# Turning the tokens of an expert's block on VectorE, from rows fetched by quarters, in a fused attention and mixture-of-experts kernel

## The chip, the cores and the metric

The kernel runs on one core of one Trainium2 chip. The metric is the device time of one execution in microseconds (us), lower is better. A profile of one execution gives, beside it, what each engine did and when: PE (TensorE matmuls), PEld (its weight loads), DVE (VectorE), ACT (ScalarE), POOL (GpSimd) and SP (SyncE, which here only issues DMAs and reads registers).

## The reference

Causal attention over 8 batches, 8 heads, 576 positions and 64 features, with a bias from a cumulative sum; its output is read as 4608 tokens of 512 features and goes through a router that sends each token to one of 8 experts:

```python
logits = x @ w_gate + modality_bias[modality_id]
e_idx = np.argmax(logits, axis=1)
...
gate_w = probs[np.arange(N), e_idx]
for e in range(E):                                  # N, D, E, F = 4608, 512, 8, 1024
    mask = e_idx == e
    h = np.maximum(x[mask] @ w1[e], 0.0)
    out[mask] = gate_w[mask, None] * (h @ w2[e])
```

All numbers are float32.

## The kernel before

**Attention** (class `Attn`, some 376 us of the span). 32 pairs of (two batches, one head) are scored, exponentiated, turned and multiplied with V. For each two batches a row of 576 floats is kept per token: 512 features, then 64 floats whose first two become the gate weight and the token's number. Routing (`Route`) scatters the rows with indirect DMAs into `lists`, a DRAM array with a region for each expert, and makes tables on the chip: `t2` with 6 blocks whose lists are filled from the first three quarters of the tokens, `t3` with 12 more, `t4` with what is left over.

**Experts** (class `Moe`). `run` goes through 18 blocks of 256 tokens of one expert (`nu` = 2), then one double block of 64 + 64 tokens (`nu` = 0, function `two`), then a loop of 64-token blocks (`nu` = 1, `quarter`), which may be empty. Each number is carried as a high and a low part in fp32r, so each product is three matmuls. For each 256-token block:

- `gather` fetches its 256 rows from `lists` into tile `xg` ([128, 2, 576], two buffers) and adds a table's entry to the token's number for the scatter at the end (`oi`, L1027).
- `xt` turns them, so that the features lie on partitions: eight TensorE transposes of 128x128 (L1039) into two PSUM tiles `tp` of one bank; for each, ACT copies the high part into `xT` (L1041) and DVE makes the low part (L1042).
- `block` makes the first layer: four groups `hp` of 24 matmuls (L1089, 256 columns), each emptied by ACT (`hT`, high, L1091) and DVE (`hT`, low, L1092); `hp` has two buffers.
- `second` makes the second layer: 48 matmuls of 512 columns into two tiles `y` (L1064); ACT (L1074) and DVE (L1072) multiply them by the gate weight from `xg` into `ys`, and POOL scatters `ys` to the output (L1075).

The weights of a block are eight chunks of 512 KB (`fetch`, L940 for w1 and L942 for w2) into six raw buffers (`wraw`, `wrbw`); ACT makes the high part (L965) and DVE the low part (L966) in 13 buffers (`wca`, `wcb`, `wcc`).

**The order.** Everything is written out in program order and each engine runs its own queue in order. While block k is multiplied, `pre(k+1)` issues the gather of block k+1 and its first two weight chunks; each of the eight `step()` calls in the block issues one more. `mid()` stands between the two layers of block k and holds `xt` of block k+1. For block 0 `xt` runs in `pre(0)`, ahead of everything else of the experts. After `xt` of block 0 the rest of the routing is emitted (`routed`), and after block 2 begins, the tables `t3` and `t4` (`R.rest`, on DVE).

All DMAs of gather and weights are issued by SP, in program order:

```python
xg, oi = self.gather(tb, b, r, nu)
x = self.xt(xg, nu) if k == 0 else None
W, self.more = self.weights(e, ...) 
```

The host passes `w1` with its 512 rows in an order that matches how `xt` takes features from the row.

Of the kernel before, what the change touches and what calls it, by code (L numbers as in the profile page):

```python
# [7 lines left out]
F32 = mybir.dt.float32  # L8
F32R = mybir.dt.float32r
BF16 = mybir.dt.bfloat16  # L10
I32 = mybir.dt.int32
AF = mybir.ActivationFunctionType
ALU = mybir.AluOpType
# [4 lines left out]
P = 128  # L18
KW = 576
XW = 72  # L20
# [18 lines left out]
class Attn:  # L39
# [166 lines left out]
    def rows(self, ho):  # L206

        nc = self.nc
        for a, (m, l) in enumerate(((0, 512), (64, 0))):
            for o, i in ((self.QL[0][64:74, a, m:m + 512].rearrange("p (c q) -> p c q", c=4), ho[64:74, :4].unsqueeze(2).broadcast_to([10, 4, P])),  # L210
                         (self.QL[0][64:74, a, l:l + 64], ho[64:74, 4:5].broadcast_to([10, 64]))):
                if a:
                    with self.tc.issue_after(self.last):
                        self.last = nc.gpsimd.tensor_scalar(o, i, 1.0, 1.0, ALU.mult, ALU.mult).ins
                else:
                    with self.tc.issue_after(self.act):
                        self.act = nc.scalar.copy(o, i).ins
# [688 lines left out]
class Moe:  # L906
# [95 lines left out]

    def gather(self, tb, b, r, nu):
        nc = self.nc
        xg = self.mx.tile([P, nu or 1, XW // 2, 8, 2], F32, name=f"xg{nu or 1}", bufs=2)
        if nu == 0:
            i = [nc.sync.dma_start(xg[64 * q:64 * q + 64, 0].rearrange("p d h r -> p (d h r)"), self.R.lists[bass.ds(r[q], 64), :]).ins for q in range(2)]
        elif nu == 2:
            i = nc.sync.dma_start(xg.rearrange("p u d h r -> p u (d h r)"),
                                  self.R.lists[bass.ds(r, 2 * P), :].rearrange("(u p) d -> p u d", u=2)).ins  # L1010
        else:
            i = nc.sync.dma_start(xg[:64, 0].rearrange("p d h r -> p (d h r)"), self.R.lists[bass.ds(r, 64), :]).ins
        if tb is self.R.t2:
            self.R.nodep(i, self.R.scat[27:])
            need = self.R.scat[:27]
        else:
            need = self.R.scat
        for i, o in ((i, o) for i in (i if nu == 0 else [i]) for o in need):
            self.tc.add_manual_dep(i, o.name, mybir.DependencyInfo(mybir.DependencyClass.Sync, mybir.DependencyReason.DATA), reason="rows of the list")
        oi = self.mp.tile([P, 2], I32, name="oi", bufs=3)  # L1020
        if nu == 0:
            for q in range(2):
                r = slice(64 * q, 64 * q + 64)
                nc.vector.tensor_tensor(oi[r, :1], xg[r, :1, 32, 0, 1], tb["past"][r, b + q], ALU.add)
            return xg, oi
        n = P if nu == 2 else 64
        nc.vector.tensor_tensor(oi[:n, :nu], xg[:n, :nu, 32, 0, 1], tb["past"][:n, bass.ds(b, 1), :].rearrange("p b u -> p (b u)"), ALU.add)  # L1027
        return xg, oi

    def xt(self, xg, nu):  # L1030
        nc = self.nc
        if nu < 2:
            return self.xq(xg) if nu else self.x2(xg)
        xT = self.mp.tile([P, 2, 4, 256], F32R, name="xT")
        for g in range(2):
            tp = self.ps.tile([P, 2, 256], F32, name="tp")
            for k in range(2):
                for u in range(2):
                    tr = nc.tensor.transpose(out=tp[:, k, P * u:P * u + P],  # L1039
                                        in_=xg[:, u, 16 * g + 8 * k:16 * g + 8 * k + 8].rearrange("p d h r -> p (d h r)"), identity=self.ident)  # L1040
            hi = nc.scalar.copy(xT[:, 0, 2 * g:2 * g + 2], tp)  # L1041
            lo = nc.vector.tensor_tensor(xT[:, 1, 2 * g:2 * g + 2], tp, xT[:, 0, 2 * g:2 * g + 2].bitcast(F32), ALU.subtract)  # L1042
        self.tr = (tr, hi, lo)
        return xT
# [13 lines left out]
    def second(self, W, xg, oi, hT):  # L1058
        nc = self.nc
        y = [self.ps.tile([P, 512], F32, name="y") for _ in range(2)]  # L1060
        for f in range(8):
            for u in range(2):
                for i, (a, c) in enumerate(self.PASS):
                    self.last[0] = nc.tensor.matmul(y[u], hT[:, a, f, P * u:P * u + P], W[4 + f // 2][:, c, 512 * (f % 2):512 * (f % 2) + 512],  # L1064
                                                    start=f == 0 and i == 0, stop=f == 7 and i == 2)
            if f % 2:
                self.step()
        for u in range(2):
            ys = self.my.tile([P, 512], F32, name="ys", bufs=3)
            gate = xg[:, u, 32, 0, 0:1]  # L1070
            if u:
                self.last[1] = nc.vector.tensor_scalar(ys, y[u], gate, None, ALU.mult)  # L1072
            else:
                self.last[3] = nc.scalar.activation(ys, y[u], AF.Copy, scale=gate)  # L1074
            self.last[2] = nc.gpsimd.indirect_dma_start(  # L1075
                out=self.out, out_offset=bass.IndirectOffsetOnAxis(ap=oi[:, u:u + 1], axis=0),
                in_=ys, in_offset=None, bounds_check=4607, oob_is_err=False)

    def block(self, W, xg, oi, xT, mid):
# [16 lines left out]
        mid()  # L1096
        self.second(W, xg, oi, hT)

    def xq(self, xg):
        nc = self.nc  # L1100
        xT = self.mp.tile([P, 2, 4, 256], F32R, name="xT")[:, 0, :, :P]
        tp = self.ps.tile([P, 4, 64], F32, name="tp")
        for k in range(4):
            nc.tensor.transpose(out=tp[:, k], in_=xg[:64, 0, 8 * k:8 * k + 8].rearrange("p d h r -> p (d h r)"), identity=self.ident[:64, :64])
        nc.scalar.copy(xT[:, :, :64], tp)
        nc.vector.tensor_tensor(xT[:, :, 64:], tp, xT[:, :, :64].bitcast(F32), ALU.subtract)
        return xT
# [13 lines left out]
    def x2(self, xg):  # L1121
        nc = self.nc
        X = self.mp.tile([P, 2, 4, 256], F32R, name="xT")[:, 0]
        tp = self.ps.tile([P, 4, P], F32, name="tp")
        for k in range(4):
            nc.tensor.transpose(out=tp[:, k], in_=xg[:, 0, 8 * k:8 * k + 8].rearrange("p d h r -> p (d h r)"), identity=self.ident)
        self.split(X, tp)
        return X

# [264 lines left out]
```

## Time and profile before

| | us |
|---|---|
| median of 3 runs | 825.9 (825.75 to 826.71) |
| the profiled execution | 826.59, of which its span is 824.9 |
| attention, to the first transpose of a block | 0 to 376.7 |
| 18 blocks | 376.7 to 802 |
| double block and end | 802 to 824.9 |
| PE busy in the three | 371.64, 424.80, 16.52 |
| DVE busy in the three | 252.78, 276.41, 11.12 |

Busy times are sums of instruction durations merged where they overlap; matmuls are pipelined, so the time a matmul takes is longer than the distance to the next one. A row of a group reads: line, engine, operation, output <- inputs, shapes, count, busy us, mean ns of one, idle time before them and what ended it. Lines are those of the kernel before.

### The profile page before, as it was taken

The page shows a single profiled execution, that of the slowest core. Times are in us where ns is not written, and L with a number is a line of the kernel's source. Part 1 is how long each engine was busy: PE and PEld are TensorE (multiplying, and loading weights), DVE is VectorE, ACT ScalarE, POOL GpSimd, SP SyncE. Part 2 cuts the span into 40 slices and gives each one's busy share as a digit, 9 for nine tenths or more (in the row PEclk, how much of TensorE's full clock was granted, in tenths as well). Part 3 has the DMA queues.
Part 4 walks back from the last instruction along what each step waited for, and adds up shares of the span by engine and source line. Part 5 has one row for each costly group of instructions (what it writes and reads, how often), then busy time and mean ns, then how long its engine had stood idle before and what let it go on. Part 6 is the DMA issues. An engine that isn't in the chain of part 4 may idle for free. (4 is left out here: it accounts for less than half of the span.)

```text
span 824.9 us, 16646 instructions
## 1 busy us (share of the span) xinstructions
PE 813.0 (99%) x5692; PEld 699.1 (85%) x5692; DVE 540.3 (66%) x1405; ACT 530.5 (64%) x1196; POOL 359.2 (44%) x383
## 2 busy tenths in 40 slices
PE   7999999999999999999999999999999999999996
PEld 7878887888887788888888899998888999988884
DVE  7666666667766677766489865555566664556874
ACT  6888788878887788876265555444455554444663
POOL 8959778988699877992500000000000000000010
PEclk7999999999999999999999999999999999999999
DMA  7565556766566656737797866655556666555970
GB/s 235 164 205 182 180 181 196 238 226 196 171 188 225 210 158 219 226 106 286 251 380 277 303 259 259 245 210 198 209 196 234 259 259 250 200 205 210 370 247 29
DMA packets 68548, 182.31 MB, mean 221 GB/s; under 512 B 7993, under 2 KB 8889, under 8 KB 68334
## 3 DMA queue, kind: packets, MB, share of 16 engines
q1 hardware_dynamic: 62622, 161.17, 57.4%
q0 software_dynamic: 5840, 20.06, 6.2%
q8 instruction: 46, 0.75, 0.4%
q14 instruction: 40, 0.33, 0.1%
HBM read 144.73 MB, written 26.80 MB: 208 GB/s over the span
## 5 line engine op out<-in xcount | busy, mean ns | idle before, releaser
L1075 POOL DMA_INDIRECT out<-ys,oi x36 | 35.9, 997 | 368.4 <-ACT ys L1074 298.5
L396 DVE CUSTOM_DVE_ANT_0 pe<-sp,mk 128x512 f32<-128x512 f32 (+3 forms) x256 | 122.4, 488 | 100.4 <-PE sp L394 92.3
L416 ACT ACTIVATE pe<-pe,mx 128x512 f32<-128x512 f32 (+3 forms) x256 | 144.3, 565 | 16.5 <-DVE mx L396 13.8
L433 PE MATMUL pt<-ident,pe 128*128 128x128 f32 x640 | 111.9, 281 | 0.1
L437 ACT COPY PT<-pt 128x512 f32<-128x512 f32 (+1 forms) x192 | 97.0, 508 | 21.2 <-PE pt L433 21.2
L372 PE MATMUL sp<-KA,QH 128*128 128x256 f32 (+2 forms) x256 | 102.6, 403 | 2.1 <-POOL KA L236 2.1
L1091 ACT ACTIVATE hT<-hp 128x512 fp32r<-128x512 f32 x72 | 42.8, 595 | 93.1 <-PE hp L1089 92.6
L474 PE MATMUL o<-PT,V 128*64 128x320 f32 (+4 forms) x896 | 100.7, 364 | 0.0
L474 PEld LDWEIGHTS o<-PT,V 128*64 128x64 f32 x896 | 58.6, 136 | 46.7 <-issue 14.7
L1089 PE MATMUL hp<-xT,wcb 128*128 128x256 f32 x648 | 89.6, 282 | 0.0
L1089 PE MATMUL hp<-xT,wca 128*128 128x256 f32 x624 | 87.3, 282 | 0.5 <-ACT xT L1041 0.5
L433 PEld LDWEIGHTS pt<-ident,pe 128*128 128x128 f32 x640 | 77.3, 145 | 12.2 <-issue 5.3
L326 POOL TENSOR_TENSOR KA<-rawk,KA 64x576 fp32r<-64x576 f32 x62 | 87.1, 1421 | 0.2
L326 POOL TENSOR_TENSOR QL<-rawq,QH 64x576 fp32r<-64x576 f32 x62 | 86.7, 1413 | 0.2
L394 PE MATMUL sp<-KB,QL 76*128 76x256 f32 (+2 forms) x256 | 85.9, 340 | 0.9 <-DMA QL<-ek 0.9
L1092 DVE SCALAR_TENSOR_TENSOR hT<-hp,hT 128x512 fp32r<-128x512 f32 x72 | 49.5, 688 | 53.2 <-ACT hT L1091 52.9
L1089 PEld LDWEIGHTS hp<-xT,wcb 128*128 128x128 f32 x648 | 83.1, 188 | 0.6
L1089 PEld LDWEIGHTS hp<-xT,wca 128*128 128x128 f32 x624 | 80.4, 188 | 1.4 <-issue 0.7
L1064 PE MATMUL y<-wcb,hT 128*128 128x512 f32 x336 | 81.2, 398 | 0.0
L1064 PEld LDWEIGHTS y<-wcb,hT 128*128 128x128 f32 x336 | 62.8, 188 | 14.7
L1089 PE MATMUL hp<-xT,wcc 128*128 128x256 f32 x456 | 64.6, 281 | 0.0
L1064 PE MATMUL y<-wca,hT 128*128 128x512 f32 x264 | 63.9, 398 | 0.0
(285 smaller groups left out, 1599.2 us busy)
## 6 DMA issues: line engine op xcount, KB each, us to landing
wrbw<-in_w SPq DMA_DIRECT2D x104, 512.0 KB
wraw<-in_w SPq DMA_DIRECT2D x56, 512.0 KB
rawq<-in_qkv SPq DMA_DIRECT2D x31, 576.0 KB
rawk<-in_qkv SPq DMA_DIRECT2D x31, 576.0 KB
xg<-lists SPq DMA_DIRECT2D x18, 576.0 KB
V<-in_qkv SPq DMA_DIRECT2D x32, 320.0 KB
KB<-KA SPq DMA_DIRECT2D x62, 144.0 KB
lists<-z SPq DMA_DIRECT2D x8, 576.0 KB
```

The costliest lines, as they stand in the source:

```text
L326: self.last = nc.gpsimd.tensor_tensor(o, i, h, ALU.subtract).ins
L372: self.pe.append(self.nc.tensor.matmul(sp[:, :nn], QH[:, q0:q0 + P], self.KA[u][:, ab, :nn], start=True, stop=False).ins)
L394: self.pe.append(nc.tensor.matmul(sp[:, :nn], QL[:EXT, q0:q0 + P], KB[:EXT, ab, :nn], start=False, stop=True).ins)
L396: ins = nc.vector.tensor_tensor_reduce(out=t[:, :n], in0=sp[:, :n], in1=self.mk[:, 512 - n:512], scale=-0.125, scalar=3.0e38, op0=ALU.add, ...
L416: self.act = nc.scalar.activation(t[:, :n], t[:, :n], AF.Exp, bias=m, scale=-1.0, accum_out=st["sums"][:, o:o + 1]).ins
L433: self.pe.append(nc.tensor.transpose(out=pt[:, o:o + P], in_=pe[:, P * j:P * j + P], identity=self.ident).ins)
L437: cp(w[:, :, :, v:v + P], pt[:, :n * (1 + both)].rearrange("p (a j q) -> p a j q", a=1 + both, q=P))
L474: m = nc.tensor.matmul(o[r, f - q0:q1 - q0], V[:, ab, j, :], PT[:, ab, PTS * j + f if j < 4 else PTW - 64:PTS * j + q1 if j < 4 else PTW], ...
L1064: self.last[0] = nc.tensor.matmul(y[u], hT[:, a, f, P * u:P * u + P], W[4 + f // 2][:, c, 512 * (f % 2):512 * (f % 2) + 512], start=f == 0 ...
L1089: nc.tensor.matmul(hp[:, u], W[k][:, a, f:f + P], xT[:, c, k], start=k == 0 and i == 0, stop=k == 3 and i == 2)
L1091: hi = nc.scalar.activation(hs, hp, AF.Relu)
L1092: lo = nc.vector.scalar_tensor_tensor(hT[:, 1, 2 * m:2 * m + 2], hp, 0.0, hs.bitcast(F32), ALU.max, ALU.subtract)
```

## The change

For 256-token blocks, `gather2` takes the place of the one DMA of `gather`. Four DMAs each fetch a quarter of the 512 features of all 256 tokens (512 bytes a token) onto 32 partitions: partition 32q + p holds, for t = 0 to 7, features 128q to 128q + 127 of token 32t + p (tile `xr`, [128, 8, 128], two buffers). A fifth DMA fetches two floats for each token, the gate weight and the number (tile `tg`, three buffers). In `xt` two VectorE instructions take the place of the eight transposes: each turns 32x32 blocks, reads every fourth feature and writes a whole `tp` tile. The gate weight and the number come from `tg`. The host orders the rows of `w1` so that feature 4d + k of a quarter meets its weight, and the transposes of the 64-token blocks (`x2`, `xq`, still on TensorE) read every fourth feature too. The 64-token gathers keep one DMA; their buffers are now of 576 floats, and `xg2` is gone.

```diff
     def gather(self, tb, b, r, nu):
         nc = self.nc
-        xg = self.mx.tile([P, nu or 1, XW // 2, 8, 2], F32, name=f"xg{nu or 1}", bufs=2)
+        if nu == 2:
+            return self.gather2(tb, b, r)
+        xg = self.mx.tile([P, 1, XW // 2, 8, 2], F32, name="xg", bufs=2)
...
-        elif nu == 2:
-            i = nc.sync.dma_start(xg.rearrange("p u d h r -> p u (d h r)"),
-                                  self.R.lists[bass.ds(r, 2 * P), :].rearrange("(u p) d -> p u d", u=2)).ins
...
+    def rows(self, tb, ins):
+
+        need = self.R.scat
+        if tb is self.R.t2:
+            for i in ins:
+                self.R.nodep(i, need[27:])
+            need = need[:27]
+        for i, o in ((i, o) for i in ins for o in need):
+            self.tc.add_manual_dep(i, o.name, ...)
+
+    def gather2(self, tb, b, r):
+
+        nc = self.nc
+        xr = self.mx.tile([P, 8, P], F32, name="xr", bufs=2)
+        tg = self.mx.tile([P, 2, 2], F32, name="tg", bufs=3)
+        rows = self.R.lists[bass.ds(r, 2 * P), :]
+        i = [nc.sync.dma_start(xr[32 * q:32 * q + 32], rows[:, P * q:P * q + P].rearrange("(t p) d -> p t d", p=32)).ins for q in range(4)]
+        i.append(nc.sync.dma_start(tg, rows[:, 512:514].rearrange("(u p) d -> p u d", u=2)).ins)
+        self.rows(tb, i)
+        oi = self.mp.tile([P, 2], I32, name="oi", bufs=3)
+        nc.vector.tensor_tensor(oi, tg[:, :, 1], tb["past"][:, bass.ds(b, 1), :].rearrange("p b u -> p (b u)"), ALU.add)
+        return (xr, tg), oi
 
     def xt(self, xg, nu):
...
         for g in range(2):
             tp = self.ps.tile([P, 2, 256], F32, name="tp")
-            for k in range(2):
-                for u in range(2):
-                    tr = nc.tensor.transpose(out=tp[:, k, P * u:P * u + P],
-                                        in_=xg[:, u, 16 * g + 8 * k:16 * g + 8 * k + 8].rearrange("p d h r -> p (d h r)"), identity=self.ident)
+            tr = nc.vector.transpose(out=tp.rearrange("p k (t n) -> p k t n", n=32),
+                                     in_=xg[0].rearrange("p t (d k) -> p k t d", k=4)[:, 2 * g:2 * g + 2])
             hi = nc.scalar.copy(xT[:, 0, 2 * g:2 * g + 2], tp)
...
-            gate = xg[:, u, 32, 0, 0:1]
+            gate = xg[1][:, u, 0:1]
...
+    def quads(self, xg, k):
+        return xg[:, 0, :32].rearrange("p d h r -> p (d h r)")[:, k::4]
...
-            nc.tensor.transpose(out=tp[:, k], in_=xg[:, 0, 8 * k:8 * k + 8].rearrange("p d h r -> p (d h r)"), identity=self.ident)
+            nc.tensor.transpose(out=tp[:, k], in_=self.quads(xg, k), identity=self.ident)
...
-    w1 = a("moe_w1").reshape(8, 8, 32, 2, 1024).transpose(0, 2, 1, 3, 4)
+    w1 = a("moe_w1").reshape(8, 8, 32, 2, 1024).transpose(0, 2, 1, 3, 4).reshape(8, P, 4, 1024).transpose(0, 2, 1, 3)
```

More of the change, by code (lines that the diff above doesn't have):

```diff
@@ L1004, in gather @@
         nc = self.nc
-        xg = self.mx.tile([P, nu or 1, XW // 2, 8, 2], F32, name=f"xg{nu or 1}", bufs=2)
+        if nu == 2:
+            return self.gather2(tb, b, r)
+        xg = self.mx.tile([P, 1, XW // 2, 8, 2], F32, name="xg", bufs=2)
         if nu == 0:
             i = [nc.sync.dma_start(xg[64 * q:64 * q + 64, 0].rearrange("p d h r -> p (d h r)"), self.R.lists[bass.ds(r[q], 64), :]).ins for q in range(2)]
-        elif nu == 2:
-            i = nc.sync.dma_start(xg.rearrange("p u d h r -> p u (d h r)"),
-                                  self.R.lists[bass.ds(r, 2 * P), :].rearrange("(u p) d -> p u d", u=2)).ins
         else:
             i = nc.sync.dma_start(xg[:64, 0].rearrange("p d h r -> p (d h r)"), self.R.lists[bass.ds(r, 64), :]).ins
[L1013 to L1019, printed above, removed]
+        self.rows(tb, i if nu == 0 else [i])
         oi = self.mp.tile([P, 2], I32, name="oi", bufs=3)
@@ L1025, in gather @@
             return xg, oi
-        n = P if nu == 2 else 64
-        nc.vector.tensor_tensor(oi[:n, :nu], xg[:n, :nu, 32, 0, 1], tb["past"][:n, bass.ds(b, 1), :].rearrange("p b u -> p (b u)"), ALU.add)
+        nc.vector.tensor_tensor(oi[:64, :1], xg[:64, :1, 32, 0, 1], tb["past"][:64, bass.ds(b, 1), :].rearrange("p b u -> p (b u)"), ALU.add)
         return xg, oi
+    def rows(self, tb, ins):
[5 more added lines that the diff above has]
+        for i, o in ((i, o) for i in ins for o in need):
+            self.tc.add_manual_dep(i, o.name, mybir.DependencyInfo(mybir.DependencyClass.Sync, mybir.DependencyReason.DATA), reason="rows of the list")
+    def gather2(self, tb, b, r):
[9 more added lines that the diff above has]
+        return (xr, tg), oi
     def xt(self, xg, nu):
@@ L1103, in xq @@
         for k in range(4):
-            nc.tensor.transpose(out=tp[:, k], in_=xg[:64, 0, 8 * k:8 * k + 8].rearrange("p d h r -> p (d h r)"), identity=self.ident[:64, :64])
+            nc.tensor.transpose(out=tp[:, k], in_=self.quads(xg[:64], k), identity=self.ident[:64, :64])
         nc.scalar.copy(xT[:, :, :64], tp)
```

## The prediction

> **What bounds the kernel.** I read the stages first: the busy time of each engine in the blocks, then who waited there, then one block in order of time.
>
> ```profile
> span 824.9 us, 16646 instructions
> 376.70:802.00 425.30, 424.80 (x2751) 385.03 (x2750) 276.41 (x385) 223.31 (x284) 46.28 (x44) 1.00 0.69 253
> 520.00:544.00 24.00, 24.00 (x156) 21.72 (x155) 14.12 (x16) 12.29 (x16) 1.97 (x2) 1.00 0.61 223
> PE hp L1089 <- ACT xT L1041: 0.5, 1, 0.5
> L1072 DVE TENSOR_SCALAR ys<-y,xg x18: 746/751/755, 402.9 to 803.2; 128x512 f32<-128x512 f32 x18
> ```
>
> Columns of the second and third row: stretch, its length, busy us of PE, PEld, DVE, ACT, POOL, granted clock, DMA share, GB/s. In the 18 blocks PE is busy 424.80 of 425.30 us at full clock; its only wait in that stage is 0.5 us, once, at the first block (fourth row). DVE has about 10 of 24 us free and DMA 39%. So PE's own work sets the pace here, and time taken from PE comes off the end as long as nobody makes PE wait. From the last row 18 blocks end 17 periods apart: (803.2 - 402.9) / 17 = 23.55 us a block.
>
> Now what the transposes cost PE: not their busy time, but the distance that they open between the two layers.
>
> ```profile
> 507.90 0.52 PE L1089 MATMUL hp<-xT,wcb 128*128 128x256 f32 x3
> 508.26 1.03 PE L1039 MATMUL tp<-ident,xg 128*128 128x128 f32 x8
> 509.05 11.48 PE L1064 MATMUL y<-wcb,hT 128*128 128x512 f32 x48
> L1039 PE MATMUL tp<-ident,xg x144: 270/272/274, 376.8 to 768.1; 128*128 128x128 f32 x144
> L1126 PE MATMUL tp<-ident,xg x4: 272/272/274, 790.9 to 791.2; 128*128 128x128 f32 x4
> ```
>
> The eight start at 508.26 and the next layer at 509.05: 0.79 us, where eight durations of 272 ns would be 2.2 us and the merged busy time 1.03; they are pipelined with what follows. The next matmul could have started at 508.26, since the three before it start 0.12 us apart (507.90 to 508.26).
>
> **Removed from PE.** 144 transposes, 18 groups: 18 x 0.79 = 14.2 us. In 17 groups the second layer simply starts earlier: its first 36 matmuls need `hT` that is long done, and the last group's low part (below, 511.58 + 0.68) is needed after 36 of 48 matmuls, at 509.05 + 36 x 11.48 / 48 = 517.7. The 18th group is the first block's (below).
>
> **Added to DVE.** Two turns a block of 128x512. No row shows this operation, so it is bounded by its neighbours.
>
> ```profile
> L745 DVE MEMSET z<- 128x576 f32 x1 | 0.5, 538 | 0.1
> L1092 DVE SCALAR_TENSOR_TENSOR hT<-hp,hT 128x512 fp32r<-128x512 f32 x72 | 49.5, 688 | 53.2 <-ACT hT L1091 52.9
> L966 DVE TENSOR_TENSOR wcb<-wrbw,wcb 128x1024 fp32r<-128x1024 f32 x39 | 47.4, 1222 | 10.1 <-ACT wcb L965 10.1
> 511.58 0.68 DVE L1092 SCALAR_TENSOR_TENSOR hT<-hp,hT 128x512 fp32r<-128x512 f32 x1
> 512.18 0.68 DVE L1042 TENSOR_TENSOR xT<-tp,xT 128x512 fp32r<-128x512 f32 x1
> 512.21 0.60 ACT L1041 CAST xT<-tp 128x512 fp32r<-128x512 f32 x1
> 515.04 0.69 DVE L1042 TENSOR_TENSOR xT<-tp,xT 128x512 fp32r<-128x512 f32 x1
> 520.37 0.88 PE L1089 MATMUL hp<-xT,wca 128*128 128x256 f32 x6
> ```
>
> Low end 0.54 (a write of 576), high end 1.22 (1024 elements, as if each element took two steps); I take 0.69, that of the 512-element instruction on the same PSUM bank size, the same shape. So +1.38 us of DVE a block, 15.5 of the new 22.76: not its bound. What matters is lateness. Now `xT` is whole at 515.73 and PE wants it at 520.37: 4.6 us spare. After: last `hT` low done 512.26; turn, ACT copy and low, twice, all in a row, with the two weight lows (1.22 each) that the trace has between the two `xT` lows still in between: 512.26 + 2 x (0.69 + 0.60 + 0.68) + 2.4 = 518.6, and PE wants it at 520.37 - 0.79 = 519.58. Covered, by 1 us in the worst order; at 1.22 a turn the same order gives 519.7, a stall of 0.1. If the cover goes, each us late is 17 us.
>
> [...]
>
> **One DMA becomes five, and a wait goes.**
>
> ```profile
> SPq L1009 <- DVE ys L1072: 170.7, 15, 18.3
> DVE oi L1027 <- DMA xg<-lists: 18.9, 15, 2.1
> L1009 SPq DMA_DIRECT2D xg<-lists x18: 372/373/403, 370.0 to 757.0; - x18
> 522.50:525.60 3.10, 3.10 (x28) 3.10 (x27) 0.69 (x1) 0.60 (x1) 0.00 (x0) 1.00 0.95 299
> q1 hardware_dynamic: 301, 0.71, 75.4%
> DMA packets 429, 0.26 MB, mean 183 GB/s; under 512 B 148, under 2 KB 412, under 8 KB 422
> 508.54 0.37 SPq L942 DMA_DIRECT2D wrbw<-in_w  x1
> 521.46 0.37 SPq L1009 DMA_DIRECT2D xg<-lists  x1
> 526.17 0.16 DVE L1027 TENSOR_TENSOR oi<-xg,rpast 128x2 int32<-128x2 f32 x1 [1.40 <-DMA xg<-lists]
> 526.96 0.69 DVE L1092 SCALAR_TENSOR_TENSOR hT<-hp,hT 128x512 fp32r<-128x512 f32 x1 [0.63 <-ACT hT L1091]
> 497.00:520.00 23.00, 23.00 (x152) 20.89 (x151) 14.04 (x16) 11.30 (x16) 1.97 (x2) 1.00 0.63 232
> ```
>
> The first row is SP's queue: the gather sits 170.7 us in 15 waits until the block two back has used its gate weight from `xg`, with the weight chunks queued behind it. `xr` is last read by the turn, a block and a half earlier, and `tg` has three buffers, so this wait goes; next late on SP is the raw weight buffer. The gather and the weights start some 170.7 / 15 = 11 us earlier in each block. SP pays four more issues of 0.37 (third row) plus their address moves, 1.6 us, out of the 11. With it should go DVE's 18.9 us of waiting for the row's number (`oi`, second row), behind which the next `hT` low stands. PE waits for neither today, so I count no gain.
>
> The packets: 256 rows become 1024 of 512 bytes and 256 of 8. The row of 301 packets is that of 522.5 to 525.6 us, mostly one gather: 3.1 us, 10.3 ns a packet. The row of 429 is that of 34.7 to 36.1 us, 1.4 us in which nearly all are under 2 KB (small saves to DRAM): 3.3 ns a packet. By packet count 1280 take 4.2 us at the second rate and 13.2 at the first; by bytes they would take 3.1 x 526/590 = 2.8, the low end. I take 4.2, since its packets are of the same size. Other transfers are busy about 0.63 x 23 - 0.754 x 3.1 = 12.2 us a block, so 16.4 of 22.76.
>
> **The first block.** Its gather cannot move ahead; it waits for the attention's space and scatters.
>
> ```profile
> 370.00:371.00 1.00, 0.91 (x8) 0.71 (x8) 0.76 (x4) 1.00 (x5) 0.92 (x2) 1.00 0.00 0
> 371.00:372.00 1.00, 1.00 (x10) 0.58 (x9) 0.40 (x3) 0.65 (x3) 1.00 (x1) 1.00 0.81 92
> 376.81 1.04 PE L1039 MATMUL tp<-ident,xg 128*128 128x128 f32 x8
> 377.56 1.07 ACT L1041 CAST xT<-tp 128x512 fp32r<-128x512 f32 x2 [1.40 <-DMA wraw<-in_w]
> 378.29 1.02 PE L1089 MATMUL hp<-xT,wca 128*128 128x256 f32 x4 [0.45 <-ACT xT L1041]
> 383.52 2.40 POOL L966 TENSOR_TENSOR wcb<-wrbw,wcb 128x1024 fp32r<-128x1024 f32 x1 [10.43 <-ACT wcb L965]
> 391.57 11.25 PE L1064 MATMUL y<-wcb,hT 128*128 128x512 f32 x47
> ```
>
> Issued at 370.0, it moves from 371.0 on. With 4.2 us for the packets and 1.6 for the issues it lands between 375.2 and 376.8. A turn (0.69) and a copy (0.6) later, 376.5 to 378.1, PE may start, against 378.29 now; but the low part and the second turn follow, 1.4 us that today ACT and DVE also need. Between a gain of 1.5 (PE free at about 376.8) and a loss of some 0.5; I take the 0.79 of the removed transposes, the middle. At 13.2 us of gather it would be +8. The weights behind it come later by the 1.6 us of issues and 1.1 of packets; the last chunk that block 0 needs is split by 385.9, and PE takes it after 391.57 (last two rows), so 5.6 us cover that.
>
> **The block where DVE is full.** Tables are made on DVE from 427 to 458 us:
>
> ```profile
> 427.40:457.70 30.30, 30.30 (x211) 28.11 (x210) 29.88 (x87) 14.86 (x19) 3.58 (x4) 1.00 0.76 272
> 454.25 0.69 DVE L1092 SCALAR_TENSOR_TENSOR hT<-hp,hT 128x512 fp32r<-128x512 f32 x1
> 455.49 0.76 PE L1089 MATMUL hp<-xT,wca 128*128 128x256 f32 x5
> ```
>
> DVE is busy 29.88 of 30.30 us, and the `hT` low that frees `hp` for PE's third group ends at 454.94, 0.55 ahead of it. Two turns (1.38) more and PE 0.79 earlier make 1.6 us of stall, or none if the weights, which come sooner, let DVE work ahead. I take +1.0.
>
> **At nothing.** The four strided transposes of the double block: at most twice their 0.6 us (four of 0.15), so up to +0.6. `w1`'s order changes no size. `oi` and the gate read a smaller tile of the same kind. Another layout of SBUF may move the first gather's wait for attention's space either way.
>
> **Sum.** -14.2 + 1.0 = -13.2. The profiled execution took 826.59 (span 824.9), so 813.4 there; against the median of 825.9, which is 0.7 lower, 812.7.
>
> **Rivals.**
> 1. *Nothing held back*: the first block gains its 1.5 and DVE works ahead in the full block: -14.9, 811.0. For it: weights come 11 us sooner. Chance 0.12.
> 2. *Turns late, a little*: a turn of 1.22, or one more weight low (1.22) ahead of the second `xT` low, brings the 518.6 to 519.7 or 519.8; 0.1 to 0.4 us of stall a block leave -11.5 to -6.4, 814.5 to 819.5. For it: DVE and ACT now wait for each other four times in this chain. Chance 0.12. [...]
> 3. *Slower by the turn*: DVE's chain ends at 517.2 + 2X for a turn of X. The 0.79 are used up at X = 1.6; at 2.4, as two passes of 1.22, PE stalls 2.4 us a block: 17 x (2.4 - 0.79) = +27, 853. Against it: the 512-element rows all lie at 0.69. Chance 0.05.
> 4. *The gather does not move ahead*, held on SP by something else: then it lands 2.7 us later than now (1.6 issue, 1.1 packets). `oi` keeps DVE to 529.0 in place of 526.3, the `hT` low behind it ends at 529.7, and the fourth `hp` group, due at 520.37 + 3 x 2.86 = 528.95 (24 matmuls of 0.119), waits 0.75 us: nearly all of the 0.79, about 825. Against it: SP issued the block's last weight chunk at 508.54 and then only waited for `ys` until 521.46. Chance 0.05.
> 5. *Slower by DMA*: at 13.2 us a gather, a block needs 12.2 + 13.2 = 25.4 us of DMA: 17 x (25.4 - 23.55) = +31 and +8 at the first block, about 865. It decides from 11.4 us a gather. Chance 0.05.
>
> The forecast (811.3 to 814.5) has 0.61. Cases 1 and 2 are faster too: 0.85 faster, 0.05 same, 0.10 slower, by 0.2% of 826, 1.7 us, which is about what a measurement of this kernel can tell. Leaving out rivals 3 to 5 the range is 810.5 to 820.
>
> **What would show it.** Right: no L1039 on PE, the second layer's first matmul 0.12 us after the last of the first; a block period of 22.76; turns of 0.6 to 0.8; no SP wait of the gather on `ys`; gather issue near the middle of the block before. Wrong: PE waiting for `xT` (DVE or ACT) at block starts, PE idle near 455, DMA share near 1 in every block, a turn over 1.2, or `oi` still waiting for its DMA.

## The result, and the profile after

| | before | after |
|---|---|---|
| median, us (range) | 826.02 (825.75 to 826.71, 4 runs) | 818.62 (818.24 to 819.81, 4 runs) |
| after / before | | 0.9912, 95% interval 0.9894 to 0.9929 |
| the profiled execution, span | 826.59, 824.9 | 818.24, 816.5 |

Of the kernel with both repairs below, one run of six is left out: 870.24 us at a mean granted clock of 0.85. Faster by 7.4 us; forecast were 13.2 (812.7), so the time lies in the range (810.5 to 820) but not in the forecast's own band (811.3 to 814.5). The gain has to be read by stage. Line numbers in rows are those of the kernel profiled. Windows of the two profiled executions, cut at the start of the last attention product (`ox`), and at first products of blocks; columns are the stretch, its length, busy us and instructions of PE, PEld, DVE, ACT, POOL, the granted clock, DMA share, GB/s. Before:

```profile
376.21:402.66 26.45, 25.95 (x174) 23.33 (x175) 17.85 (x37) 14.15 (x23) 11.75 (x10) 1.00 0.63 238
402.66:449.79 47.13, 47.13 (x306) 42.75 (x305) 37.58 (x81) 25.85 (x33) 4.69 (x5) 1.00 0.94 347
449.79:520.37 70.58, 70.58 (x457) 63.99 (x456) 47.95 (x71) 36.76 (x47) 6.24 (x6) 1.00 0.66 244
520.37:779.40 259.03, 259.03 (x1674) 234.92 (x1672) 156.28 (x179) 131.94 (x167) 21.63 (x22) 1.00 0.64 236
```

After:

```profile
375.56:403.63 28.07, 25.50 (x159) 22.89 (x159) 22.13 (x41) 14.31 (x23) 13.53 (x10) 0.94 0.80 257
403.63:448.73 45.10, 45.10 (x289) 40.76 (x288) 37.81 (x90) 21.62 (x28) 4.67 (x5) 1.00 0.83 299
448.73:524.20 75.47, 70.54 (x434) 63.01 (x432) 53.79 (x68) 37.13 (x48) 8.18 (x6) 0.98 0.77 252
524.20:771.47 247.27, 246.64 (x1585) 222.94 (x1584) 184.40 (x208) 136.97 (x174) 22.44 (x22) 1.00 0.79 251
```

The rows are the first block, two blocks, the three blocks behind the making of the tables, and eleven blocks up to the start of the last one. Against the forecast's terms (0.79 for each group of eight transposes, +1.0 for the tables' block):

| stage | forecast | measured |
|---|---|---|
| up to 376 us | 0 | -0.65 (375.56 - 376.21) |
| first block, to the second block's start: two groups | -1.58 | **+1.62** |
| two blocks | -1.58 | -2.03 |
| three blocks behind the tables | -2.37 + 1.0 = -1.37 | **+4.89** |
| eleven blocks | -8.69 | **-11.76** |
| last block and end (span less 779.40, 771.47) | 0 | -0.47 |
| sum | -13.2 | -8.4 |

So two places lose 9.5 us against the forecast, and the steady blocks win 3 us that nobody had promised: three places, one of them on the good side. What PE waited for from 376 us on (us in all, times, longest), the new instruction (shortest, median, longest ns), and what ACT waited for:

```profile
PE hp L1102 <- ACT xT L1054: 3.3, 2, 2.5
PE hp L1102 <- DVE xT L1055: 2.9, 1, 2.9
PE hp L1102 <- DVE wcc L966: 1.1, 2, 0.6
PE hp L1102 <- DVE hT L1105: 0.6, 1, 0.6
L1052 DVE STREAM_TRANSPOSE tp<-xr x36: 1072/1104/1143, 376.7 to 743.5; 128x512 f32<-128x512 f32 x36
ACT xT L1054 <- DVE tp L1052: 34.9, 25, 4.8
```

The turn takes 1.10 us, between the 0.69 taken and the high end of 1.22. By the last row ACT waits for it 34.9 us in 25 waits; PE waits little outside the two bad places. SP's part went as forecast, here in a steady block with its window:

```profile
605.06 1.89 SPq L1038 DMA_DIRECT2D xr<-lists  x4
590.98:613.58 22.60, 22.60 (x145) 20.45 (x144) 15.73 (x18) 11.63 (x16) 1.97 (x2) 1.00 0.82 269
```

These rows are turned in the next block, which starts at 613.58. So the fetch goes 8.5 us ahead of the start of the block that turns it, where it went 1.1 us behind it before (521.46 against 520.37): 9.6 us earlier, and the forecast had 11 less 1.6. PE is busy through the whole block. The DMA share is 0.82, 18.5 us of the block where the forecast had 16.4.

### The profile page after: what moved, and what is told of

Read it like the earlier page. It is cut to its first block, busy times and chain, and to the rows that moved or that the text cites. A ratio compares the mean times of both kernels' runs of the same rounds, so it can differ in the third digit from the quotient of the medians.

```text
span 816.5 us, 16747 instructions
## 1 busy us (share of the span) xinstructions
PE 796.9 (98%) x5548; PEld 681.4 (83%) x5548; DVE 575.3 (70%) x1441; ACT 529.7 (65%) x1196; POOL 364.4 (45%) x383
## 5 line engine op out<-in xcount | busy, mean ns | idle before, releaser
L1088 POOL DMA_INDIRECT out<-ys,oi x36 | 39.0, 1084 | 357.1 <-ACT ys L1087 264.8
L1102 PEld LDWEIGHTS hp<-xT,wcc 128*128 128x128 f32 x456 | 59.3, 191 | 6.3 <-DVE xT L1055 3.1
```

What stands on the lines that cost most here:

```text
L1102: nc.tensor.matmul(hp[:, u], W[k][:, a, f:f + P], xT[:, c, k], start=k == 0 and i == 0, stop=k == 3 and i == 2)
```

## The experiments

Times are medians; ratios are to the kernel before, run beside each on the same chip. The order of each engine's queue is fixed when the kernel is built; "traced with priority" below changes that order and nothing else.

### The three blocks behind the tables: not the turn's length

Three edits. The turn ahead in VectorE's queue:

```python
+        with self.tc.high_priority(offset=300):
             for g in range(2):        # turn, ACT's copy and the low part
                 ...
```

> The changed kernel with one edit: the turn, its ACT copy and its low are traced at a higher priority, so that VectorE's queue has both turns together, ahead of the low parts and of most table work; nothing else moves. Theory (the turn's place in VectorE's in-order queue made the 28.80 us block): the block from 448.73 us takes 22.6 to 24, and the kernel 812.5 to 814.5 us. Rival A (VectorE simply has too much to do from 427 to 458 us, whatever the order): the weights' lows are late in place of the turn, that block still takes 26 or more, 816 to 818.6 us. Rival B (the transfers in quarters are what holds the block): unchanged, 818.6 us.

The tables' work in two parts:

```python
-                        if k == 2:
-                            for _ in R.rest(): pass
+                        if k == 2: ...     # R.rest() up to the t3 tables
+                        if k == 3: ...     # the remainder
```

> The changed kernel with the tables' VectorE work cut in two: the tables of the t3 blocks stay in the third block's stretch, those of the t4 blocks move one block later. The turn keeps its priority. Theory (place in the queue): both turns now stand ahead of the lows in the full block, which takes 22.6 to 24; 812.5 to 814.5 us, about as the run with the turn first. Rival A (too much work in all): the work is spread over two blocks, so it gains here too, and more than the run with the turn first, which leaves the work where it was. Rival B (transfers): unchanged, 818.6 us.

No turn at all (this kernel leaves the turning out, so its products are of data that is not turned):

```python
-            tr = nc.vector.transpose(out=tp..., in_=xg[0]...)
+            tp = xg[0][:, 4 * g:4 * g + 4].rearrange("p (k u) d -> p k (u d)", k=2)
```

> The changed kernel without the turn in the blocks of 256 rows: the high and low parts are made straight from the fetched rows, so the products are of data that is not turned; everything else, the transfers too, is as changed. It shows what the turn's 36 instructions cost in all. Theory: 810 to 812 us, the full block at 22.6 to 23.5, the first block 1 to 1.5 us shorter. Rival A (VectorE has too much work there even without 2.2 us of turns): the full block stays above 25, 815 to 817 us. Rival B (transfers or TensorE itself): 817 to 818.6 us.

| run | us (range) | ratio, 95% | three blocks |
|---|---|---|---|
| turn first | 817.43 (816.32 to 818.09) | 0.9880 to 0.9911 | 74.18 |
| tables in two parts | 818.38 (817.01 to 819.44) | 0.9899 to 0.9926 | 74.69 |
| no turn | 814.74 (814.30 to 815.11) | 0.9849 to 0.9879 | 75.35 |

The last column is the length of the same three blocks, 75.47 as changed. Row of the run without a turn:

```profile
446.35:521.70 75.35, 71.63 (x433) 63.14 (x432) 46.20 (x58) 36.87 (x48) 7.81 (x6) 0.98 0.79 261
```

As changed, PE's longest wait in these blocks is for the low part of the second turn:

```profile
454.77 0.68 DVE L1055 TENSOR_TENSOR xT<-tp,xT 128x512 fp32r<-128x512 f32 x1
455.51 1.09 PE L1102 MATMUL hp<-xT,wcc 128*128 128x256 f32 x4 [2.86 <-DVE xT L1055]
455.70:459.10 3.40, 3.40 (x17) 3.40 (x17) 3.40 (x4) 0.00 (x0) 0.35 (x1) 0.50 1.08 239
```

That is the turn's place in the queue, as my theory had it, and from 455.70 us the granted clock is 0.50 for 3.4 us (last row). But the theory as the whole cause fell. With the turn first this wait is gone and the clock stays at 1.00, yet PE waits for other things, the block from 449.41 us still takes 27.34 us, and the time lies in rival A's range. With the tables in two parts rival A misses too: the second part stands ahead of `hT` lows in the next block, and PE waits 4.0 us for one. That time is rival B's (unchanged), but by this wait and not by transfers. And without any turn, with PE's transposes gone just the same, the stretch is as long as with it (the block behind the tables takes 26.42 us); what that run gains, it gains elsewhere (2.0 us in the first block, below), and its 814.74 us misses my range and, narrowly, rival A's. The queues show what happened. Before, ACT's two casts of `wca` and the first of VectorE's two lows:

```profile
438.37 1.04 ACT L965 CAST wca<-wraw 128x1024 fp32r<-128x1024 f32 x1
439.78 1.06 ACT L965 CAST wca<-wrbw 128x1024 fp32r<-128x1024 f32 x1
439.82 1.22 DVE L966 TENSOR_TENSOR wca<-wraw,wca 128x1024 fp32r<-128x1024 f32 x1
```

As changed:

```profile
442.75 1.08 DVE L1052 STREAM_TRANSPOSE tp<-xr 128x512 f32<-128x512 f32 x1
443.87 0.59 ACT L1054 CAST xT<-tp 128x512 fp32r<-128x512 f32 x1 [4.76 <-DVE tp L1052]
444.36 1.05 ACT L965 CAST wca<-wraw 128x1024 fp32r<-128x1024 f32 x1
446.48 1.22 DVE L966 TENSOR_TENSOR wca<-wraw,wca 128x1024 fp32r<-128x1024 f32 x1
```

Without a turn:

```profile
438.86 1.05 ACT L965 CAST wca<-wrbw 128x1024 fp32r<-128x1024 f32 x1
444.60 1.21 DVE L966 TENSOR_TENSOR wca<-wraw,wca 128x1024 fp32r<-128x1024 f32 x1
```

Before, seven table instructions stand in VectorE's queue between the last `hT` low of the block and the first `wca` low. As changed 18 stand ahead of the turn and 29 ahead of that low, ACT's copy waits 4.76 us for that turn, and ACT's casts stand behind the copy. Without a turn 30 table instructions and the lows of xT stand ahead of it, and the lows of `wca` run 5 to 6 us after their casts, with VectorE never idle and no wait shown: the order keeps them. Either way the first low is at 444.6 or 446.5 instead of 439.8, and what stands behind it in the queue is late as well. With the turn first (30 tables ahead of the low, which starts at 449.0), PE's waits from 440 to 524 us show the same lateness under another name:

```profile
PE hp L1103 <- DVE wcc L966: 1.5, 3, 0.6
PE hp L1103 <- DVE wca L966: 1.0, 2, 0.6
```

So these counts and waits point to the tables that stand ahead of all the work with a deadline, whichever of turn and lows comes last; the turn's length does not cost these 6 us, nor does its place alone. The stretch without a turn holds time at half the clock too (0.50 from 452 to 454 us). Why the build ordered the two kernels differently was not tried.

### The first block: the turn's place and the clock

The first block alone fetched in whole rows and turned by TensorE:

```python
+            return self.gather2(...) if self.n > self.NA else self.gather1(tb, b, r)
...
+            if len(xg) == 3:
+                for k in range(2):
+                    for u in range(2):
+                        tr = nc.tensor.transpose(out=tp[:, k, P * u:P * u + P],
+                             in_=xg[2][:, u, :512][:, 2 * g + k::4], identity=self.ident)
```

> The changed kernel with the first block alone fetched in whole rows and turned by TensorE (8 transposes with a step of 16 bytes), all other blocks as changed. Theory (in the first block the turn waits behind VectorE's last attention work, TensorE stands idle for 2.45 us and then gets a lower clock): the first hp product starts about 0.5 us earlier, the granted clock does not drop to 0.5 after it, and the kernel takes 817.0 to 817.8 us. Rival (the first block's loss is not the turn's): 818.3 to 819 us, with the same low clock.

815.82 us (815.39 to 818.33), ratio 0.9862 to 0.9892: 2.8 us below the changed kernel, where I expected 0.8 to 1.6. As changed (timeline, then windows):

```profile
375.56 0.76 PE L346 MATMUL ox<-pw,oT 128*128 128x144 f32 x4 [0.47 <-ACT oT L477]
376.35 0.46 DVE L497 TENSOR_TENSOR x<-ox,rs 128x288 f32<-128x288 f32 x1 [1.37 <-PE ox L346]
376.72 1.08 DVE L1052 STREAM_TRANSPOSE tp<-xr 128x512 f32<-128x512 f32 x1
378.77 0.36 PE L1102 MATMUL hp<-xT,wca 128*128 128x256 f32 x1 [2.45 <-ACT xT L1054]
380.00:382.00 2.00, 2.00 (x13) 2.00 (x13) 1.97 (x4) 2.00 (x3) 0.00 (x0) 0.65 1.30 201
380.60:384.00 3.40, 3.40 (x19) 3.40 (x18) 3.37 (x7) 1.87 (x3) 0.00 (x0) 0.50 1.13 292
382.00:384.00 2.00, 2.00 (x12) 2.00 (x11) 1.97 (x6) 0.47 (x2) 0.00 (x0) 0.50 0.98 348
384.00:386.00 2.00, 2.00 (x19) 2.00 (x19) 2.00 (x6) 1.49 (x3) 0.56 (x1) 1.00 1.04 414
```

With the first block on TensorE:

```profile
378.33:403.66 25.33, 24.87 (x167) 22.12 (x167) 19.97 (x39) 14.34 (x23) 11.82 (x9) 1.00 0.84 259
378.93 1.11 PE L1063 MATMUL tp<-ident,xg 128*128 128x128 f32 x8
380.45 0.47 PE L1115 MATMUL hp<-xT,wca 128*128 128x256 f32 x2 [0.41 <-ACT xT L1067]
382.00:384.00 2.00, 2.00 (x20) 2.00 (x19) 2.00 (x3) 1.69 (x3) 0.00 (x0) 1.00 1.29 204
```

VectorE idles 1.37 us, then does the last attention work (L497), and only then the turn. It was not the rows that were late. From 370 to 374 us (first row below) 1024 packets have between 512 bytes and 2 KB, the four quarters of 256 rows, and from 374 to 376.5 us (second row) none has. So they had landed 2.7 us ahead of the turn, and earlier than the 375.2 of the forecast:

```profile
DMA packets 1401, 0.62 MB, mean 154 GB/s; under 512 B 336, under 2 KB 1360, under 8 KB 1400
DMA packets 497, 0.97 MB, mean 388 GB/s; under 512 B 23, under 2 KB 23, under 8 KB 497
```

PE stands 2.45 us, and 1.8 us after it resumes (378.77) its granted clock falls to 0.50, for the 3.4 us from 380.60 to 384.00: 12 products in 2 us where the other kernel makes 20. TensorE's own transposes filled that gap, so PE stood 0.41 us and its clock stayed at 1.00. The stretch is 25.33 instead of 28.07 us. In the run without a turn PE stood 0.92 us there, the clock stayed at 1.00 and the stretch took 26.06. So 2.45 us of standing was followed by 0.50, and 0.92 us was not. But in the same run without a turn two waits of 1.00 and 0.49 us near 450 us were followed by 0.50, so the length of one wait does not settle it.

### Fewer tables in one place

The t4 tables, not needed before the last block, five blocks later (`k == 8`), once with the turn as it is and once with the first block on TensorE too.

```python
                         if k == 2: ...     # R.rest() up to the t3 tables
+                if k == 8: ...             # the remainder, behind M.hold and M.last[1]
```

> The changed kernel with the VectorE work of the t4 tables (some 7 us, not needed before the last block) moved from the block that starts near 426 us to the one that starts near 569 us; the turn keeps its priority and its place. The runs before spoke for rival A: with the turn first the lows of the weights came late instead, and without any turn the full block still took 26.4 us. Theory now (between two weights' deadlines VectorE has 16.4 us of tables where only about 7 us are free in a block): the block after the tables takes 22.6 to 24 instead of 28.80 us, and the kernel 813 to 815 us, with at most 1 us lost at the new place. Rival (the place of the turn in the queue, not the amount of work): the turn still stands behind 14 table instructions, ACT's copy waits some 4 us for it, the weights' casts behind that copy stay late, and the block stays above 26 us; 816.5 to 818.6 us.

> The changed kernel with both repairs: the t4 tables late and the first block turned by TensorE. If the two losses are separate, as the theory has it, the gains add: 2.8 us (measured for the first block alone) and 4 to 5.5 us, so 810 to 812 us. Rival (one loss hides the other, or VectorE stays the bound in the full block): 814 to 816 us.

Tables late: 815.55 us (814.92 to 817.26), ratio 0.9853 to 0.9882. Both: 812.97 (812.02 to 814.06, 5 runs), 0.9828 to 0.9854. With the tables late:

```profile
450.18:473.53 23.35, 22.79 (x146) 20.22 (x144) 14.89 (x17) 10.87 (x15) 1.97 (x2) 1.00 0.85 295
450.18:523.27 73.09, 69.82 (x433) 61.49 (x432) 50.45 (x56) 36.36 (x47) 6.75 (x6) 1.00 0.76 260
473.73 0.75 DVE L1085 TENSOR_SCALAR ys<-y,tg 128x512 f32<-128x512 f32 x1 [4.52 <-PE y L1077]
474.40 1.22 DVE L966 TENSOR_TENSOR wcb<-wraw,wcb 128x1024 fp32r<-128x1024 f32 x1
475.67 0.97 PE L1102 MATMUL hp<-xT,wcb 128*128 128x256 f32 x6 [1.01 <-DVE wcb L966]
```

The block behind the tables takes 23.35 us instead of 28.80 (448.73 to 477.53), as the theory had it, although ACT still waits 3.9 us for the turn. The first `wca` low starts no earlier than as changed (447.10 against 446.48), but only 14 table instructions stand ahead of it instead of 29, and both turns with their lows are done by 446.84, where the second low of xT ended at 455.45: less table work was the cure, and all the rest moved up. But the three blocks still take 73.09 us, not 68.3 (three times 22.76), and the times of both runs lie 0.6 and 1 us above the ranges that I expected. The last three rows show one reason: VectorE stands 4.52 us at `ys`, with a weight's low queued behind it that PE then waits for. Moving that low ahead of `ys` was not tried. The two repairs add up: 2.80 and 3.07 us alone, 5.65 together.

### Steady blocks: 64 bytes

Nothing in the forecast explains blocks of 22.1 us. The change made the fetched rows' tiles smaller, so everything behind them in the state buffer, xT and hT among it, moved down by 928 bytes. Undone with a gap:

```python
+        self.nc.gpsimd.memset(self.mx.tile([P, 232], F32, name="gap", bufs=1)[:, :1], 0.0)
```

> The changed kernel with 928 bytes per partition left free ahead of the fetched rows, so that the weights' low buffers, xT and hT lie at the addresses that they had before the change. It tests why steady blocks take 22.1 to 22.7 us where 22.76 was expected, the products with the wca and wcc weights being 0.1135 us apart and not 0.119. Theory (where the operands lie in the state buffer sets that distance): back to 0.119 in those blocks, 0.3 to 0.5 us a block more in about half of them, 821 to 823 us. Rival (the distance comes from what else runs at that time, transfers or VectorE): unchanged, 818.2 to 819 us.

822.81 us (821.05 to 827.84, 12 runs), ratio 0.9948 to 0.9978: of the 7.4 us, 4.2 went with the addresses. By stage in the profiled executions, the eleven steady blocks take 250.27 us instead of 247.27 and the five blocks ahead of them 0.6 more. The first block takes 29.06 instead of 28.07, with a mean granted clock of 0.88 instead of 0.94, and that 1 us is not the products' pace. First-layer products counted in 10 us (first number in brackets); as changed with `wca`, as changed with `wcb`, and at the old addresses with `wca`:

```profile
524.20:534.20 10.00, 10.00 (x89) 10.00 (x89) 1.00 1.05 322
546.30:556.30 10.00, 10.00 (x84) 10.00 (x84) 1.00 0.99 336
525.10:535.10 10.00, 10.00 (x84) 10.00 (x84) 1.00 1.04 325
```

PE is busy throughout in all three; only the pace differs, and DMA share and GB/s do not go with it. Which relation of addresses? First guess, xT and the weights alike to a multiple of 64, tried on the kernel before (a gap of 32 bytes ahead of xT) and on the changed kernel with both repairs (two gaps of 32 bytes):

```python
+        self.nc.gpsimd.memset(self.mp.tile([P, 8], F32, name="gap", bufs=1), 0.0)     # both
+        self.nc.gpsimd.memset(self.wr.tile([P, 8], F32, name="gapw", bufs=1), 0.0)    # the second, ahead of wcb
```

> The kernel before with one edit that computes nothing: 32 bytes per partition are left free ahead of xT and hT, so that these lie, like all weight buffers, 32 bytes past a multiple of 64. In the runs so far the hp products were 0.1135 us apart where xT and the weights lay alike to a multiple of 64 (the changed kernel with wca and wcc) and 0.119 where they differed by 32 (its wcb, and everything with the old addresses). Theory (it is this relation): 96 products by 0.0055 us, 0.5 us a block in 18 blocks, so 816 to 818 us without any of the change. Rival (it is the place in the buffer otherwise, or needs the change's transfers): 825.5 to 826.5 us.

> The changed kernel with the t4 tables late, the first block turned by TensorE, and two gaps of 32 bytes that put xT, hT and all weight buffers 32 bytes past a multiple of 64. Theory (the relation of the addresses sets the distance of the products): the blocks of 22.4 to 22.7 us go to 22.1, some 4 to 5 us in all below the 813.2 of the run with the two repairs: 808 to 810 us. Rival (not the relation): 813 us.

824.15 us (822.70 to 825.52, 10 runs), 0.9960 to 0.9981, and 815.35 (814.78 to 816.79), 0.9851 to 0.9887: the guess is wrong, and the second kernel is slower than without its gaps. (The first gains 1.7 us all the same, with first layers as long as before; that is not explained.) The addresses of all runs, to a multiple of 128, leave one candidate:

| run | xT | wca, wcc | wcb | products in 10 us |
|---|---|---|---|---|
| before, old addresses | 64 | 96 | 96 | 84 |
| before with 32 bytes; all repairs | 96 | 96 | 96 | 84, 85 |
| as changed; late and first | 32 | 96 | 64 | **89** with wca, 84 with wcb |

One layer speaks against it: as changed, the block whose weights are all `wcc`, 64 bytes apart too, has 85.

```profile
681.76:691.76 10.00, 10.00 (x85) 10.00 (x85) 1.00 0.66 206
```

> The run with all repairs, with the second gap 96 bytes instead of 32, so that xT and hT lie 32 bytes past a multiple of 128 and all weight buffers 96 past one, that is 64 bytes apart to a multiple of 128. The relation to a multiple of 64 has failed: alike by it, the products of the run with all repairs were no faster. What the short blocks (hp layer 10.9 us) of all runs so far have in common is this distance of 64 to a multiple of 128; at distances of 0 and 32 the layer took 11.3 to 11.5. Theory (it is this distance): the hp layer takes 10.9 in all steady blocks, their periods 22.0 to 22.2, and the kernel 808 to 811 us. Rival (another property of the old places): 11.4 to 11.5 in most blocks, 813 to 816 us.

```python
-        self.nc.gpsimd.memset(self.mp.tile([P, 8], F32, name="gap", bufs=1), 0.0)
+        self.nc.gpsimd.memset(self.mp.tile([P, 24], F32, name="gap", bufs=1), 0.0)
```

**807.25 us** (806.86 to 809.40, 5 runs), ratio 0.9766, 0.9749 to 0.9782: the fastest of all, 19.0 us below the kernel before (826.29 beside it) and 8.1 below its twin with 64 bytes less. Its windows with `wcb` alone, with `wca` and `wcc`, and one exception:

```profile
541.95:551.95 10.00, 10.00 (x89) 9.99 (x88) 1.00 1.02 349
564.00:574.00 10.00, 10.00 (x89) 10.00 (x89) 1.00 0.93 335
519.45:529.45 10.00, 10.00 (x85) 9.99 (x85) 1.00 1.04 333
541.95:741.32 199.37, 198.51 (x1298) 179.74 (x1297) 156.98 (x198) 112.50 (x144) 19.91 (x18) 1.00 0.79 255
```

`wcb` is fast too now; nine blocks take 22.15 us on the mean, with one of 23.45 in them. The block at 519.45 is at the slow pace at the same addresses, like the `wcc` block above, so something else can take the gain away; that stays open. And only one pair of places was fast, xT at 32 and weights at 96 to a multiple of 128, so whether the distance decides or this pair is not shown.

### One part alone: the gate's own tile

The kernel before with the gate and the token number fetched a second time into `tg`, so that the rows' buffer is free after the transposes. First with three buffers for `tg` and `oi`, then with four, and with a gap of 32 bytes.

```python
+            tg = self.mx.tile([P, 2, 2], F32, name="tg", bufs=3)     # second run: 4, and oi 4
+            j = nc.sync.dma_start(tg, self.R.lists[bass.ds(r, 2 * P), 512:514]...).ins
```

> The kernel before with one part of the change alone: the gate and the token number are fetched a second time into a small tile of their own (one more DMA a block), so that the fetched rows are free as soon as TensorE has turned them and the next fetch goes earlier; rows whole, transposes on TensorE. Theory (TensorE's instruction stream sets the block; the earlier fetch is worth nothing by itself): 825.5 to 826.5 us. Rival A (the earlier fetch is what made the steady blocks shorter than expected): 819 to 823 us. Rival B (the extra DMA and the earlier fetch delay weights): 827 us or more.

> The kernel before with the gate and the token number fetched into a small tile of their own (one more DMA a block), now with four buffers for that tile and for oi instead of three, and with 32 bytes left free so that xT and hT stay at a multiple of 64 as before. With three buffers VectorE's oi stood 64.7 us waiting in 12 blocks and the run took 866.6 us, so it did not test the earlier fetch. Theory (the earlier fetch alone is worth nothing, TensorE sets the block): 825 to 827 us. Rival A (the extra DMA and the fetch's new place among the weights' cost time by themselves): above 830 us. Rival B (the earlier fetch is itself a gain): 820 to 824 us.

The first took 866.57 us (859.78 to 869.46, 6 runs), 1.0443 to 1.0506, the second 824.98 (823.93 to 828.75, 12 runs), 0.9974 to 1.0000. Lines of the first:

```profile
581.93 0.37 SPq L1029 DMA_DIRECT2D tg<-lists  x1
590.79 0.16 DVE L1034 TENSOR_TENSOR oi<-tg,rpast 128x2 int32<-128x2 f32 x1 [5.65 <-DMA out<-ys,oi]
590.87 1.28 DVE L1104 SCALAR_TENSOR_TENSOR hT<-hp,hT 128x512 fp32r<-128x512 f32 x2
591.61 0.62 PE L1101 MATMUL hp<-xT,wca 128*128 128x256 f32 x3 [2.39 <-DVE hT L1104]
```

With the row buffers free, the rows were fetched about a block earlier. Three buffers were then too few: `tg` was fetched only behind a `ys`, and `oi`, an instruction of 0.16 us, stood 5.65 us in VectorE's queue until an earlier scatter had read its buffer, with two `hT` lows behind it, and PE waited for those. The run is 40 us longer. PE's waits for `hT` lows are 28.7 us of it, and the rest is about what the lower granted clock costs, 0.981 on the mean where the second run has 0.997: an estimate of 14 us (0.016 of 865). With four buffers the fetch goes a block and 2.5 us ahead of the start of the block that turns it (540.31 to 542.83, and then 566.31) where it went 1.1 us behind it before (520.37 to 521.46), and that is worth 1 us by the medians, 0 to 2.1 by the interval: near the nothing of the forecast. Even this 1 us may not be the fetch's: with the gap xT starts at 0 to a multiple of 128, and at 64 before.

The first of these runs also has the places of the kernel as changed (xT at 32, `wca` at 96), on TensorE's transposes. Its block with `wca` alone does 72 products in 8.64 us (from 526.37), 0.12 us each, so there these places were not fast.

## Why the prediction was right, and where it was wrong

- **"Removed from PE", 0.79 us a group: right.** At the old addresses the ten blocks from 525.09 us take 22.765 us on the mean, where 22.76 was written:

```profile
525.09:752.74 227.65, 227.04 (x1441) 204.84 (x1440) 170.24 (x192) 124.87 (x160) 22.46 (x20) 1.00 0.76 249
```

- **"Added to DVE", 0.69 us a turn: mis-sized (1.10), without effect.** It lies in the time that `xT` had to spare, and in steady blocks PE does not wait for it; by the sum of rival 3 a turn of 1.10 ends the chain at 519.4, ahead of 519.58. At a step of 16 bytes the turn took 1.6 times the 0.69. No run turns without that step, so its share is not shown. Rival 2 gives the right size of time by the wrong cause: steady blocks lost nothing. No run shows the 0.4 us of stall a block that ends its range at 819.5, and with it the forecast's at 820: the turns took 1.10 us, and PE did not wait for them in steady blocks.
- **"One DMA becomes five": right.** The waits on `ys` and of `oi` went, the fetch moved ahead, and the second run of the gate alone puts that at about nothing. Rivals 4 and 5 did not come.
- **"The first block", +0.79 gained: wrong.** It put the first product after the landing of the rows, which came earlier than it said, and no row of it was VectorE's queue, where attention's last L497 stands ahead of the turn. The turn cost 2.7 us there, the time at half the clock included, and the stretch came out 3.2 us longer than forecast.
- **"The block where DVE is full", +1.0: wrong, the largest miss (6.3 us).** The step added 1.38 us of turns to VectorE's work and kept the order of its queue. The order changed, the lows of two weights and the second turn went behind the tables, and ACT's casts behind a copy that waits for the turn. PE waited 2.86 us for the second turn's low, and 3.4 us at a granted clock of 0.50 followed. The run without turns shows that the length of the turn did not matter.
- **"At nothing": wrong in one word, the layout.** The text let it move only a wait. The run without the shift of 928 bytes is 4.2 us longer; at equal addresses the change gains 3.2. The strided transposes of the double block, priced at up to +0.6, do not show: the end is 0.47 shorter.

The sign held even at the old addresses, but that the time fell into the range is luck: a gain that was not foreseen covered part of two losses, and without it the kernel takes 822.81 us, above the range's 820.

## What to carry to other kernels

When a step moves from one engine's in-order queue to another's, ask at the fullest and at the first place of that queue what will stand ahead of it and what behind, on the engine that consumes it as well; its duration was the smaller question (three blocks of 75.35 us without the turn, 75.47 with it). A change that alters the size of a tile can move the tiles behind it, here by 928 bytes, worth 4.2 us: give the experiment a gap that puts them back, or the layout's share is taken for the change's. Work without a deadline (the t4 tables) belongs where its engine has room.

## What was not expected of the hardware

- Products of 128x256 in float32r ran at 89 in 10 us in most layers where xT and the weights start 64 bytes apart to a multiple of 128 (85 in two others), and at 84 or 85 at distances of 0 and 32. Two gaps of 32 and 96 bytes were worth 5.7 us on an otherwise equal kernel (812.97 to 807.25), and 64 bytes more of one of them 8.1 (815.35 to 807.25). What in the buffer does it was not tested.
- PE standing 2.45 us was followed by a granted clock of 0.50 for 3.4 us, from 1.8 us after it resumed; 2.86 us was followed by 0.50 for 3.4 us too, from 0.2 us after it resumed, and two waits of 1.00 and 0.49 us near each other by 0.50 from 452 to 454 us of the run without a turn. After standing 0.92 or 0.41 us the clock stayed at 1.00.
- One buffer too few for two small tiles, `tg` and `oi`, cost 40 us, through an instruction of 0.16 us.
